# Nine transfers in place of one in a stream of weights, and four table rows on another queue

## The chip, the cores and the metric

The kernel runs on one core of a Trainium2 chip. The metric is the device time of one execution in microseconds (us); lower is better. Before the change the median of three runs is 419.34 us (419.34 to 419.83).

A core has five engines that the text speaks of by the names the profile gives them: PE (TensorE, matrix products), DVE (VectorE) and ACT (ScalarE) for elementwise work, POOL (GpSimd), and SP (SyncE), which here only issues transfers. Transfers between memory and the core's on-chip memory run on 16 DMA engines; an instruction on SP or POOL issues one, and it is then moved while the issuing engine goes on.

## The reference, cut to what matters

Linear attention with an elu feature map, followed by a spectral mixing layer: a real Fourier transform over the sequence, a complex 512 by 512 product for each of the 64 lowest modes, the inverse transform, and a channel product.

```python
def _attn_ref(q, k, v):                     # q, k, v: (8, 8, 576, 64) float32
    phi = lambda x: np.where(x > 0, x, np.exp(x) - 1.0) + 1.0
    q_p, k_p = phi(q), phi(k)
    kv = np.einsum('bhsd,bhse->bhde', k_p, v)
    z = np.sum(k_p, axis=2)
    num = np.einsum('bhsd,bhde->bhse', q_p, kv)
    den = np.einsum('bhsd,bhd->bhs', q_p, z)[..., None] + 1e-06
    return num / den

def _moe_ref(x, w_r, w_i, w_ch):            # x: (8, 576, 512); w_r, w_i: (64, 512, 512)
    X = np.fft.rfft(x, axis=1)
    Xr, Xi = np.real(X[:, :64]), np.imag(X[:, :64])
    Yr = np.einsum('bmd,mde->bme', Xr, w_r) - np.einsum('bmd,mde->bme', Xi, w_i)
    Yi = np.einsum('bmd,mde->bme', Xr, w_i) + np.einsum('bmd,mde->bme', Xi, w_r)
    Y = np.zeros_like(X); Y[:, :64] = Yr + 1j * Yi
    u = x + np.fft.irfft(Y, n=576, axis=1)
    return u + np.maximum(u @ w_ch, 0.0)
```

The weights `w_r` and `w_i` are 134 MB in float32, by far the largest input. They are read once and turned into bfloat16 on the way.

## The kernel before, in words

**Stages.** The first stage (about 0 to 113 us) does the attention of the eight batches and the forward transform. For each batch `load` (L169) brings q, k and v, `exps` and `features` build the feature maps, `turn_q` transposes q, `sum_kv` sums the products of k and v, `form_x` divides, `transform` multiplies by the forward table `fwd_sb`, and `place_x` puts the spectra where the mode products need them. The second stage (about 113 to 389 us) goes over the 64 modes in 32 pairs: `mode_pair(p)` (L528) multiplies the spectra by the weights of modes 2p and 2p + 1, 16 matmuls on one tile `P` (L498), and copies, picks and stores the result on chip. Between the pairs PE does slices of other work (`work_slot`): the attention rows again in float32, the inverse transform of the early modes, the channel product, and filler matmuls (`keep_warm`, L485). The last stage (to 418 us) adds the late modes and stores the output.

**The weights' transfers.** `w_load(p, half, ...)` (L104) issues one transfer on POOL: the real weights of a pair (half 0) or the imaginary ones (half 1). The tile has 128 rows; one half takes every other row, so a transfer is 64 rows of 16 x 512 elements, 16 KB each as bfloat16. A pair is multiplied when both its halves have landed. Five pairs (two in `wpool`, three in `wpre`) are loaded during the first stage, by `w_next` among the batches' loads. Later pairs go through `wpool` with two buffers: `w_get(p)` (L474) issues both halves of pair p once the products of pair p - 2, which had the buffer, are done. The last pair is loaded in pieces (`w_load_last`, L114).

**Queues and order.** Nearly all issues are in a hand-written order (`pin`), which holds for each engine. POOL issues k and v of batch 0, then q, k and v of batch 1, then makes the identity and the turning matrices (L311), then issues q of batch 2 and so on. SP issues q of batch 0 in two transfers (L177), then the forward table (L179): only 81 of its rows are stored, and `fold_table` (L324) makes the others on PE from these by symmetry, at 11.95 us and after, between `turn_q(0)` and `sum_kv(0)`. The stores of the last stage are SP's too.

**Completion counters.** Each transfer counts up a counter (a semaphore) when it has landed. The program as built gives POOL's transfers eight such counters in turn.

Of the kernel before, what the change touches and what calls it, by code (L numbers as in the profile page):

```python
# [33 lines left out]
def kernel(  # L34
# [10 lines left out]
    nc = tc.nc  # L45
# [6 lines left out]
    NJJ = 4  # L52
    NDW = 4 * NDC
# [12 lines left out]
    FROWS = S // 4 - 63  # L66
    fwd_dr = nc.inline_tensor(np.ascontiguousarray(fwd_np[:FROWS, :4]), name="dft_fwd")
# [6 lines left out]
    fwd_sb = const.tile([128, 5, 2 * NM], F16, name="fwd_sb")  # L74
# [23 lines left out]
    pin = tc.keep_in_program_order  # L98
# [2 lines left out]

    LAST = NM // 2 - 1

    def w_load(p: int, half: int, pool, tag: str, bufs: int):  # L104
        if half == 0:
            w_in[p] = pool.tile([128, NDW, D], BF16, tag=tag, bufs=bufs, name=f"w{p}")
        two = (moe_w_r, moe_w_i)[half][2 * p : 2 * p + 2]
        pin(
            nc.gpsimd.dma_start(  # L109
                out=w_in[p][half::2], in_=two.rearrange("g (r dc) e -> (g r) dc e", dc=NDW)  # L110
            )
        )

    def w_load_last(pool, tag: str, bufs: int):  # L114
        w_in[LAST] = pool.tile([128, NDW, D], BF16, tag=tag, bufs=bufs, name=f"w{LAST}")
# [23 lines left out]
    def w_next():  # L139
        p, half = pending.pop(0)  # L140
        pool, tag, bufs = (wpool, "w", W_KEEP) if p < n_keep else (wpre, "wp", W_PRE)
        w_load(p, half, pool, tag, bufs)
# [26 lines left out]
    def load(b):  # L169
        for nm, src in (("q", q), ("k", k), ("v", v)):  # L170
            rows_in = src[b].rearrange("h s d -> (h s) d").rearrange(
                "(hp r j) d -> r hp (j d)", r=128, j=2 * NJ
            )
            if (nm, b) == ("q", 0):
                for c in range(2):
                    t = sA.tile([128, 2, NJ * Dh], F32, tag="x16", bufs=2, name=f"q32_{c}")
                    pin(nc.sync.dma_start(out=t, in_=rows_in[:, :, c * NJ * Dh : (c + 1) * NJ * Dh]))  # L177
                    raw[nm, b, c] = t
                pin(nc.sync.dma_start(out=fwd_sb[0:FROWS, 0:NJJ, :], in_=fwd_dr.ap()))  # L179
                continue  # L180
            t = sA.tile([128, 2, 2 * NJ * Dh], F16, tag=f"{nm}16", bufs=2, name=f"{nm}16_{b}")
            pin(nc.gpsimd.dma_start(out=t, in_=rows_in))
            raw[nm, b] = t

    def heads(nm, b, c):
        if (nm, b) == ("q", 0):
            return raw[nm, b, c].rearrange("p o (j d) -> p o j d", d=Dh)
        return raw[nm, b].rearrange("p o (c j d) -> p c o j d", c=2, d=Dh)[:, c]
# [219 lines left out]
    def transform(b, dc):  # L408
# [17 lines left out]
        if dc == NDC - 1:  # L426
# [3 lines left out]
            pin(nc.scalar.mul(out=xv[:, :, 0, :], in_=xf[:, :, 1, :], mul=-SPEC))  # L430

    load(0)
    load(1)
    ones_where(id16, -1, 1, 0)
    make_turns()
# [4 lines left out]
    for b in range(B):  # L440
        if b + 2 < B:
            load(b + 2)
            if b % 2 == 1:
                w_next()
        turn_q(b, 0)
        turn_q(b, 1)
        if b == 0:
            fold_table()
        sum_kv(b)
        if b + 1 < B:  # L450
            for _ in features(b + 1):
                pass
        if b + 2 < B:
            exps(b + 2)
        for jj in range(NJJ + 1):
            form_x(b, jj)
            if b == 0 and jj == 0:
                make_place()
            if b > 1 and jj == 1:
                place_x(b - 2)  # L460
            if b > 0 and jj in (2, 3):
                transform(b - 1, jj - 2)
        if b > 0:
            transform(b - 1, 2)
            transform(b - 1, 3)
# [8 lines left out]
    def w_get(p: int):  # L474
        if p not in w_in and p == LAST:
            w_load_last(wpool, "w", W_KEEP)
        elif p not in w_in:
            for half in range(2):
                w_load(p, half, wpool, "w", W_KEEP)
        return w_in[p]  # L480
# [189 lines left out]
    def x_of(t: int):  # L670
        if t < B * NJJ:
            return x_main[t // NJJ][:, t % NJJ, :]
        i = t - B * NJJ
        return x_tail[i // 2][:, i % 2, :]
# [458 lines left out]
    def sums_of(n: int, tiles_of):  # L1133
        channels(n, tiles_of)
        add_inverse(n, 1, tiles_of)
        for i in tiles_of:
# [6 lines left out]
            out=x_of(0), in0=accs[0][:, 0], scalar=0.0, in1=x_of(0), op0=ALU.max, op1=ALU.add  # L1143
# [51 lines left out]
```

## Time and profile before

| what | us |
| --- | --- |
| median of three runs | 419.34 (419.34 to 419.83) |
| the profiled execution, whole | 419.94 |
| its span, first to last instruction | 418.2 |
| busy: PE / DVE / ACT / POOL | 295.0 / 240.2 / 153.2 / 61.3 |
| issue to landing, `w` from `in_moe_w_r_dram`, median | 12.5 |
| issue to landing, `w` from `in_moe_w_i_dram`, median | 16.8 |

The page that follows in parts comes from one profiled execution. Its third part lists the DMA queues: q0 holds what POOL issues, q1 what SP issues, q8 and q14 the fetches of instructions. Its fourth part is the chain of work that ended last, followed back from the end. A line of the fifth part reads: source line, engine, operation, tile written and tiles read, shape and count, then busy time and the mean of one in ns, then the idle time of that engine just before these instructions and what ended most of it. A line of the timeline reads: start, duration, engine, source line, operation, tiles, count, and in brackets the idle time before it and what ended it.

### The profile page before, as it was taken

What the parts mean: (1) busy time and instruction counts of PE and PEld (TensorE: products, weight loads), DVE (VectorE), ACT (ScalarE), POOL (GpSimd) and SP (SyncE); (2) the same over time, 40 slices, a digit from 0 to 9 for tenths busy, and PEclk for the clock granted to TensorE, in tenths of its full rate; (3) what the DMA queues carried; (4) which work ended last, traced back from release to release, by engine and by line L of the source; (5) the groups of instructions that cost most, each with busy time, mean ns of one, the idle gap of its engine ahead of it and who ended that gap; (6) DMA issues with size and microseconds to landing.
All of it is one profiled execution on the core that took longest, in us unless ns stands there. A gap on an engine that the chain in (4) does not pass through costs nothing.

```text
span 418.2 us, 6982 instructions
## 1 busy us (share of the span) xinstructions
PE 295.0 (71%) x2890; PEld 158.9 (38%) x2890; DVE 240.2 (57%) x533; ACT 153.2 (37%) x226; POOL 61.3 (15%) x110
## 2 busy tenths in 40 slices
PE   0279999999674455444435676978796967998992
PEld 0167777777411222212122232333342422453431
DVE  4779879995437474455536453564454534522794
ACT  4667767954200001000000233334352522331682
POOL 6222222300020111111111111111111111130200
PEclk9999999989755655556665589999897988899997
DMA  8999999999999999999999999999999999998698
GB/s 216 212 212 214 211 219 205 222 215 220 212 215 218 213 221 212 216 217 216 218 216 215 219 212 216 218 215 217 216 215 218 215 215 219 215 210 172 210 401 344
DMA packets 16564, 92.86 MB, mean 222 GB/s; under 512 B 2069, under 2 KB 2790, under 8 KB 12374
## 3 DMA queue, kind: packets, MB, share of 16 engines
q0 software_dynamic: 12656, 81.53, 93.8%
q1 hardware_dynamic: 3878, 10.90, 6.9%
q8 instruction: 22, 0.36, 0.3%
q14 instruction: 8, 0.07, 0.0%
HBM read 163.66 MB, written 9.44 MB: 414 GB/s over the span
## 4 chain that ended last, share of the span: by engine, by line
DMA 55%; PE 25%; DVE 10%; ACT 3%; issue 3%; POOL 3%; ACTq 0%; POOLq 0%
DMA w<-in_moe_w_i_dram 52%; PE P L498 5%; PE kvp L258 5%; DVE x_main L965 4%; DMA k<-in_k_dram 3%; DVE x L294 3%; PE xf L417 2%; PE qTp L238 2%; PE xp L385 2%; POOL w L109 2%; PE num L156 1%; PE zl L485 1%; PE z L858 1%; ACT qT L245 1%; PE xf L422 1%
## 5 line engine op out<-in xcount | busy, mean ns | idle before, releaser
L498 PE MATMUL P<-w,xz 128*32 128x512 bf16 x496 | 49.2, 537 | 71.7 <-DMA w<-in_moe_w_i_dram 69.4
L109 POOL DMA_DIRECT2D w<-in_moe_w_r_dram x31 | 17.2, 553 | 247.9 <-PE P L498 246.2
L515 ACT CAST ys<-P 128x512 f16<-128x512 f32 x15 | 8.8, 586 | 118.1 <-PE P L498 112.3
L498 PEld LDWEIGHTS <-xz 128*32 128x32 bf16 x496 | 12.9, 117 | 93.8 <-DMA w<-in_moe_w_i_dram 77.3
L513 DVE CAST ys<-P 128x512 f16<-128x512 f32 x17 | 11.8, 692 | 58.0 <-PE P L498 58.0
L838 PE MATMUL eps<-wch,xTw 128*128 128x512 f16 x144 | 42.0, 420 | 0.0
L819 DVE TENSOR_TENSOR x_main<-ya,x_main 128x512 f32<-128x512 f32 x32 | 22.0, 689 | 20.5 <-PE ya L815 20.3
L821 ACT CAST x16w<-x_main 128x512 f16<-128x512 f32 x32 | 19.8, 618 | 37.1 <-DVE x_main L819 35.4
L258 PE MATMUL kvp<-vpad,ke 32*128 32x130 f16 x576 | 24.0, 265 | 8.5 <-ACT qT L245 8.5
L846 ACT CAST E<-eps 128x512 f16<-128x512 f32 (+1 forms) x40 | 21.2, 540 | 22.4 <-PE eps L838 22.4
L769 PE MATMUL nw<-kv_diag,qT 128*128 128x130 f16 (+1 forms) x160 | 24.6, 297 | 6.4 <-DVE x_tail L782 3.2
L258 PEld LDWEIGHTS <-ke 32*128 32x128 f16 x576 | 22.2, 117 | 10.0 <-issue 9.6
L508 DVE COPY xz<-xt_c 64x256 bf16<-64x256 bf16 x62 | 22.9, 369 | 2.2 <-PE P L498 1.4
L294 DVE TENSOR_TENSOR x<-num,rd 128x512 f16<-128x512 f32 x32 | 22.1, 691 | 1.1
L238 PE MATMUL qTp<-id,qe 128*128 128x128 f16 x144 | 15.2, 289 | 10.1 <-DVE qe L222 9.6
L769 PEld LDWEIGHTS <-qT 128*128 128x128 f16 (+1 forms) x160 | 14.5, 134 | 19.9 <-issue 11.4
L156 PE MATMUL num<-kv_sb,qT 64*128 64x65 f16 (+1 forms) x320 | 16.3, 219 | 5.7 <-DVE x L294 3.3
L245 ACT COPY qT<-qTp 128x1152 f16<-128x1152 f16 x16 | 19.6, 1293 | 2.0 <-PE qTp L238 1.5
L782 DVE TENSOR_TENSOR x_main<-nw,rd 128x256 f32<-128x256 f32 x32 | 11.2, 415 | 15.8 <-PE nw L769 15.8
L830 DVE COPY xTw<-xTp 128x512 f16<-128x512 f16 x36 | 15.0, 416 | 6.8 <-PE xTp L828 6.8
L838 PEld LDWEIGHTS <-xTw 128*128 128x128 f16 x144 | 13.7, 107 | 11.8 <-issue 4.7
L204 ACT ACTIVATE ke<-k 128x2304 f16<-128x2304 f16 x8 | 16.9, 2112 | 2.6 <-DMA k<-in_k_dram 2.6
(153 smaller groups left out, 525.2 us busy)
## 6 DMA issues: line engine op xcount, KB each, us to landing
w<-in_moe_w_r_dram POOLq DMA_DIRECT2D x31, 1024.0 KB, 12.5
w<-in_moe_w_i_dram POOLq DMA_DIRECT2D x31, 1024.0 KB, 16.8
out_dram<-x_main SPq DMA_DIRECT2D x14, 512.0 KB, 3.5
k<-in_k_dram POOLq DMA_DIRECT2D x8, 576.0 KB, 12.0
v<-in_v_dram POOLq DMA_DIRECT2D x8, 576.0 KB, 12.4
q<-in_q_dram POOLq DMA_DIRECT2D x7, 576.0 KB, 11.7
q<-in_q_dram SPq DMA_DIRECT2D x2, 576.0 KB, 4.4
w<-in_moe_w_r_dram POOLq DMA_DIRECT2D x2, 512.0 KB, 11.5
```

The costliest lines, as they stand in the source:

```text
L109: nc.gpsimd.dma_start(out=w_in[p][half::2], in_=two.rearrange("g (r dc) e -> (g r) dc e", dc=NDW))
L156: mm = nc.tensor.matmul(num[hpo][orow, c0 : c0 + 65], qT[rows, hpp, h2, cols], kv_sb[rows, hpp, h2, :])
L238: nc.tensor.transpose(qT_ps[:, j], phi["q", b][:, c, j].rearrange("p o d -> p (o d)"), id16,)
L245: nc.scalar.copy(out=qT[:, :, c * NJ : (c + 1) * NJ], in_=qT_ps.rearrange("p j x -> p x j"))
L258: nc.tensor.matmul(kv_ps[:, h2, 0:130], phi["k", b][r0 : r0 + 32, j // NJ, j % NJ].rearrange("p o d -> p (o d)"), vp[r0 : r0 + 32, :, j, 0 ...
L294: nc.vector.tensor_tensor(out=dst.rearrange("p (o c d) -> p o c d", o=2, c=4), in0=nv[:, :, :, 0:64], in1=rden.unsqueeze(3).broadcast_to([ ...
L498: nc.tensor.matmul(P[c : c + n, :], x, w[:, dc, :], start=(dc < NDC), stop=(dc >= n_dc - NDC), tile_position=(0, c), skip_group_check=True,)
L508: pin(nc.vector.tensor_copy(out=xz[p % 2][HALVES[h], :, h, :], in_=src))
L769: nc.tensor.matmul(num[c][orow, h2 * 130 : h2 * 130 + 130], qT[:, c, h2, rows_of(jj, BASE[b % 2])], kv_diag[:, b, c, h2].rearrange("p o n ...
L819: pin(nc.vector.tensor_tensor(out=x, in0=acc, in1=x, op=ALU.add))
L838: nc.tensor.matmul(e_ps, xT[:, c, :], wch16[:, c, :], start=(c == 0), stop=(c == NDC - 1))
L846: pin(nc.scalar.copy(out=dst, in_=e_ps[:, cols]))
```

## The change

Two edits. In the first, `W_SHARES` names one half of one pair, the imaginary weights of pair 24, and `w_load` issues it as nine transfers: one of 48 rows and eight of 2 rows. All other halves stay one transfer of 64 rows. In the second, SP's transfer of the forward table carries 77 rows in place of 81, and the other four are issued by POOL, right behind v of batch 0.

```diff
+    W_SHARES = {(24, 1): (48,) + (2,) * 8}
+
     def w_load(p: int, half: int, pool, tag: str, bufs: int):
         if half == 0:
             w_in[p] = pool.tile([128, NDW, D], BF16, tag=tag, bufs=bufs, name=f"w{p}")
         two = (moe_w_r, moe_w_i)[half][2 * p : 2 * p + 2]
-        pin(
-            nc.gpsimd.dma_start(
-                out=w_in[p][half::2], in_=two.rearrange("g (r dc) e -> (g r) dc e", dc=NDW)
-            )
-        )
+        rows_in, r0 = two.rearrange("g (r dc) e -> (g r) dc e", dc=NDW), 0
+        for n in W_SHARES.get((p, half), (64,)):
+            pin(nc.gpsimd.dma_start(out=w_in[p][half::2][r0 : r0 + n], in_=rows_in[r0 : r0 + n]))
+            r0 += n
...
-                pin(nc.sync.dma_start(out=fwd_sb[0:FROWS, 0:NJJ, :], in_=fwd_dr.ap()))
+                pin(nc.sync.dma_start(out=fwd_sb[0 : FROWS - 4, 0:NJJ, :], in_=fwd_dr.ap()[0 : FROWS - 4]))
                 continue
             t = sA.tile([128, 2, 2 * NJ * Dh], F16, tag=f"{nm}16", bufs=2, name=f"{nm}16_{b}")
             pin(nc.gpsimd.dma_start(out=t, in_=rows_in))
             raw[nm, b] = t
+            if (nm, b) == ("v", 0):
+                r = slice(FROWS - 4, FROWS)
+                pin(nc.gpsimd.dma_start(out=fwd_sb[r, 0:NJJ, :], in_=fwd_dr.ap()[r]))
```

## The prediction

> **What bounds the kernel now.** I read the page first, for the engine that never rests and the chain that ends last.
>
> ```profile
> span 418.2 us, 6982 instructions
> ...
> DMA  8999999999999999999999999999999999998698
> ...
> q0 software_dynamic: 12656, 81.53, 93.8%
> q1 hardware_dynamic: 3878, 10.90, 6.9%
> q8 instruction: 22, 0.36, 0.3%
> ...
> DMA 55%; PE 25%; DVE 10%; ACT 3%; issue 3%; POOL 3%; ACTq 0%; POOLq 0%
> ...
> L498 PE MATMUL P<-w,xz 128*32 128x512 bf16 x496 | 49.2, 537 | 71.7 <-DMA w<-in_moe_w_i_dram 69.4
> L109 POOL DMA_DIRECT2D w<-in_moe_w_r_dram x31 | 17.2, 553 | 247.9 <-PE P L498 246.2
> ```
>
> The DMA row stands at 9 from the second slice to the 36th, and 55% of the chain is transfers: from 117 to 389 us the kernel is one stream of weights on GpSimd's queue, and TensorE waits for it (69.4 of L498's 71.7 us of idle time). Whatever delays this stream delays the end; the 28 us behind it are a fixed tail. Next the timeline of TensorE and GpSimd around pair 24, whose second half is cut up:
>
> ```profile
> 299.28 1.05 PE L498 MATMUL P<-w,xz 128*32 128x512 bf16 x16 [2.47 <-DMA w<-in_moe_w_i_dram]
> ...
> 300.65 0.54 POOL L109 DMA_DIRECT2D w<-in_moe_w_r_dram  x1 [8.57 <-PE P L498]
> 301.19 0.55 POOL L109 DMA_DIRECT2D w<-in_moe_w_i_dram  x1
> ...
> 309.10 1.05 PE L498 MATMUL P<-w,xz 128*32 128x512 bf16 x16 [1.02 <-DMA w<-in_moe_w_i_dram]
> ...
> 310.46 0.54 POOL L109 DMA_DIRECT2D w<-in_moe_w_r_dram  x1 [8.73 <-PE P L498]
> ...
> 318.78 1.90 PE L498 MATMUL P<-w,xz 128*32 128x512 bf16 x16 [3.34 <-DMA w<-in_moe_w_i_dram]
> ```
>
> Pair 22 is multiplied at 299.28, its buffer is free at 300.65, and pair 24 is issued there. Pair 23 lands at 309.10 and pair 25 is issued at 310.46, while pair 24 is still moving until 318.78: the queue holds about 8 us of work whenever an issue comes, so it never empties. That reserve is what the change can spend.
>
> The trace's DMA records (one per packet) add two things. A row of a half is one packet of 16 KB and 1.227 us, four rows per engine, and successive halves complete 4.85 us apart. And the 16 engines are not level: the completion marks of one transfer lie 0.7 us apart at the start, 3.28 us at pair 24, 3.65 us at the last pairs. The 22 instruction fetches of q8 (16 KB, 0.89 to 0.98 us each) each go through one engine and, as I read it, leave it behind. A landing is that of the slowest engine.
>
> Last, how GpSimd's transfers wait for each other. In the program as built they take eight completion counters in turn, and a transfer waits until the former user of its counter, eight transfers earlier, has landed, unless something before it proves that. The trace has this wait:
>
> ```profile
> 74.70 0.58 POOL L109 DMA_DIRECT2D w<-in_moe_w_r_dram  x1
> 76.52 0.74 POOL L109 DMA_DIRECT2D w<-in_moe_w_i_dram  x1 [1.25 <-DMA q<-in_q_dram]
> 78.93 0.54 POOL L109 DMA_DIRECT2D w<-in_moe_w_r_dram  x1 [1.67 <-DMA k<-in_k_dram]
> 81.70 0.54 POOL L109 DMA_DIRECT2D w<-in_moe_w_i_dram  x1 [2.23 <-DMA v<-in_v_dram]
> ```
>
> The buffers of these weights are free; what ends each wait is a q, k or v load issued eight transfers before. It costs nothing there, because the queue is full.
>
> **The table's four rows.** SP's third transfer shrinks from 81 to 77 rows; GpSimd gets a transfer more, between v of batch 0 and q of batch 1. Nearest rows for its issue: 0.60 us (the four-row L1118, 1.20 for two) and 0.73 us (the q, k, v loads). So q, k and v of the next batch, two `affine_select`s' worth of work (L311) and q of batch 2 are issued up to 0.7 us later. These loads sit behind a queue that lands one load per 2.79 us from 9.4 us on (k of batch 1 is issued at 3.60 and lands at 17.72), so nothing is late. The rows themselves land behind v of batch 0, at about 12.3 us, where the first table matmul (L330) ran at 11.95: TensorE starts it 0.3 us later, covered because VectorE takes the result only at 14.45, behind v's copy (L228), and TensorE's next work is at 21.07. The packets cost the stream 0.05 us. From both sides: -0.1 to +0.7 if that cover failed. I take 0.
>
> **The cut half.** Removed: one issue of 0.55 us and 64 rows. Added: nine issues, the same 64 rows. Bytes are equal, and I take the 16 pieces' rows as evenly spread, so each engine still has 3 + 1 rows. Issues: the four-piece row of L121 has 2.21 us for four, so 0.55 each; GpSimd idles 8.7 us here. What is new are the waits. As built, pieces 1 to 4 wait for nothing, piece 5 for pair 23's first half (304.2), piece 6 for its second (309.1), piece 7 for pair 24's first half (318.78 - 4.85 = 313.93), and piece 8 for the 48-row transfer itself. Behind piece 8 on GpSimd stands pair 25, which was issued at 310.46 before. So:
>
> 1. The 48 rows land one row before the old landing: 318.78 - 1.23 = 317.55.
> 2. GpSimd wakes 0.25 us after TensorE for the same landing (rows below: 377.82 and 378.07): piece 8 is issued at 317.80.
> 3. Pair 25's first half follows one issue later, at 318.35, instead of 310.46.
> 4. From the start of an issue to its first packet on an empty queue: 1.56 us (L1067) and 1.66 (L1118), issue rows below against the DMA records. I take 1.6: 319.95.
> 5. Piece 8's own row: 317.80 + 1.6 + 1.23 = 320.63, so pair 24 lands there, 1.85 late, and two engines start pair 25 at 320.63.
>
> ```profile
> 377.82 1.05 PE L498 MATMUL P<-w,xz 128*32 128x512 bf16 x16 [0.60 <-DMA w<-in_moe_w_i_dram]
> 378.07 0.55 POOL L121 DMA_DIRECT2D w<-in_moe_w_i_dram  x1 [4.04 <-DMA w<-in_moe_w_i_dram]
> ...
> 387.49 0.64 POOL L1067 DMA_DIRECT2D YZ_all<-rows_ahead  x1 [8.88 <-DMA w<-in_moe_w_i_dram]
> ...
> 389.89 1.20 POOL L1118 DMA_DIRECT2D YZ_all<-last_z  x2 [1.76 <-ACT last_z L1113]
> ```
>
> The slowest engine had begun pair 25 at 318.78; the most advanced one at 318.78 - 3.28 = 315.50. All now begin at 319.95: 1.17 late for the slowest, 4.45 for the most advanced. The engines are level again, which takes away the lag of the past, and the lag to come starts from zero: fetches at 329.9, 352.0 and 376.1 us put 0.9 to 0.95 on one engine each, where before they raised the spread only from 3.28 to 3.65. End of the stream: 4.45 + 0.95 - 3.65 = +1.75 us; with a fetch on one of piece 8's engines +2.4. What follows is late by the same: pair 26 waits for pair 24's products, issued 2 us later, with pair 25 moving until 329.7, so no second gap. TensorE's surplus waits for nine counters are some 0.04 us each (the POOLq semaphore instructions) and long satisfied. I take **+1.8 us**.
>
> Step 4 is the least known. Nearest rows on both sides: 1.43 us (SP's first issue at 0.81, first packet at 2.24) and 4.5 us (GpSimd's first load, issued 1.33, first packet 5.86, at start-up). I take the two of the tail, whose queue was warm and empty. That gives +1.6 to +4.7. The Trainium skill, "DMA: Bandwidth & Descriptors", section "Latency and other measured facts", puts the first byte from GpSimd at about 1 us; by that figure the sum would be +1.2. This trace says 1.6.
>
> On the profiled execution, 418.2 us of span and 419.94 in all (1.7 around it), that is 421.7; it lies 0.6 over the median of 419.34, on which I put the forecast: 419.34 + 1.8 = **421.1 us**.
>
> **Rivals.**
> - *The gap is hidden*: same. If waking, two issues and the first packet together take under 2 us instead of 2.4, and later fetches strike engines that are not last, the sum is at most +0.8: 419.3 to 420.1. For it: the slowest engine has only 1.17 us of gap. Against it: the same steps measured in the tail.
> - *Two engines take all pieces.* If each two-row transfer goes to the same two engines, these have 3 + 8 rows. A most advanced engine ends them at 314.30 + 8 x 1.23 = 324.1 (piece 8 arrives at 319.4, in time): +5.4, less 0.4 of lag, 424.3; the slowest one: +8.6, 427.9. The records show four-row transfers starting on four engines (the tail's L1118), but not whether the next one takes other engines. The Trainium skill, same page, "Why a DMA increments its semaphore by 16 and not by 1", describes both: engines in turn from a cursor, and an exception with a fixed ceil(rows/16) per engine; the second would give this rival, and no row here decides.
> - *The cut spares the slowest engine*: faster. If the pieces miss the engine that is 3.28 us behind, it has three rows instead of four, and pair 24 could land at 317.55. It decides only if pair 25's first packet is there 1.23 us after the 48 rows, that is if piece 8 doesn't wait for them; then the stream gains 1.2: 418.1. Against it: the wait is in the program as built, and eight times two rows are just 16 engines.
> - *Every piece pays its own start.* If the eight pieces went one behind the other at 0.25 + 0.55 + 1.6 + 1.23 = 3.6 us, the last seven would cost 25 us: 444. Against it: halves complete 4.85 us apart, with no start between them, and six pieces are queued early.
>
> **How the numbers follow.** Forecast 0.74, hidden 0.10, two engines 0.09, faster 0.05, every piece 0.02. The forecast's own range is 420.4 to 422.4; the 8-in-10 range takes in half of the hidden case, the long first packet and the cheaper end of the two engines: 419.9 to 424.4. A change of 0.2% (0.84 us) is about what can be told from none: faster 0.05, same 0.11, slower 0.84.
>
> **What would show it.** In the changed trace: GpSimd's eighth piece and pair 25 issued near 318 us with a wait for the imaginary weights, instead of 310.5; a dip in the DMA row at 318 to 320; pair 24's products at about 320.6 and pair 25's near 330 instead of 328.5; the spread of completion marks under 1 us behind pair 24; the tail equally long. I am wrong if pair 25 is issued at 310.5, if the DMA row has no dip, if marks of two engines come some 5 us behind the rest, or if the first table matmul's delay reaches VectorE.

## The result, and the profile after

The changed kernel takes 426.17 us (median of 4 runs, 425.81 to 426.6) against 419.36 before (4 runs, 419.34 to 419.83): a ratio of 1.016, 95% interval 1.0143 to 1.0178. That is 6.8 us slower, where 1.8 was forecast, and it lies outside the forecast range (419.9 to 424.4).

The page of the changed kernel, the lines that answer to those of before:

```profile
span 423.8 us, 6998 instructions
...
DMA  8999999999999999999999999999978999998598
...
q0 software_dynamic: 12928, 81.54, 92.7%
...
DMA 59%; PE 19%; DVE 10%; issue 4%; ACT 3%; POOL 3%; ACTq 0%; POOLq 0%
...
L502 PE MATMUL P<-w,xz 128*32 128x512 bf16 x496 | 49.5, 540 | 78.7 <-DMA w<-in_moe_w_i_dram 76.5
...
L112 POOL DMA_DIRECT2D w<-in_moe_w_r_dram x31 | 17.1, 553 | 236.5 <-PE P L502 233.7
```

The span grew by 5.6 us. TensorE's idle time before the products (L502, formerly L498) grew by 7.0, all of it waiting for imaginary weights, and the DMA row, level before, has a dip (7, 8) in slices 30 and 31, that is from 307 to 328 us. The timeline there, the products of pairs 22 to 25 and GpSimd's issues; TensorE's other work between them is left out:

```profile
299.79 1.05 PE L502 MATMUL P<-w,xz 128*32 128x512 bf16 x16
301.15 0.54 POOL L112 DMA_DIRECT2D w<-in_moe_w_r_dram  x1 [7.80 <-PE P L502]
301.69 2.53 POOL L112 DMA_DIRECT2D w<-in_moe_w_i_dram  x5
304.84 0.51 POOL L112 DMA_DIRECT2D w<-in_moe_w_i_dram  x1 [0.62 <-DMA w<-in_moe_w_r_dram]
309.47 1.90 PE L502 MATMUL P<-w,xz 128*32 128x512 bf16 x16 [2.00 <-DMA w<-in_moe_w_i_dram]
309.71 0.50 POOL L112 DMA_DIRECT2D w<-in_moe_w_i_dram  x1 [4.36 <-DMA w<-in_moe_w_i_dram]
314.60 0.50 POOL L112 DMA_DIRECT2D w<-in_moe_w_i_dram  x1 [4.39 <-DMA w<-in_moe_w_r_dram]
318.24 0.64 POOL L112 DMA_DIRECT2D w<-in_moe_w_i_dram  x1 [3.14 <-DMA w<-in_moe_w_i_dram]
318.87 0.56 POOL L112 DMA_DIRECT2D w<-in_moe_w_r_dram  x1
319.42 0.55 POOL L112 DMA_DIRECT2D w<-in_moe_w_i_dram  x1
325.18 1.90 PE L502 MATMUL P<-w,xz 128*32 128x512 bf16 x16 [7.90 <-DMA w<-in_moe_w_i_dram]
...
334.62 1.05 PE L502 MATMUL P<-w,xz 128*32 128x512 bf16 x16 [1.02 <-DMA w<-in_moe_w_i_dram]
```

The waits are those that were forecast: the last pieces are issued one by one, each behind a landing, and pair 25 at 318.87 in place of 310.46. But pair 24 is multiplied only at 325.18, 6.9 us after the issue of its last piece began. The windows of the same execution show what moves meanwhile (columns: stretch, length, busy time and count of PE, weight load, DVE, ACT and POOL, clock, DMA share, GB/s):

```profile
314.00:316.00 2.00, 2.00 (x18) 1.32 (x16) 1.74 (x6) 1.10 (x2) 0.50 (x1) 1.00 0.49 99
316.00:318.00 2.00, 1.28 (x7) 0.33 (x4) 2.00 (x5) 0.74 (x2) 0.00 (x0) 1.00 0.22 41
318.00:320.00 2.00, 0.00 (x0) 0.00 (x0) 0.77 (x3) 0.88 (x2) 1.74 (x3) 0.86 0.16 33
320.00:322.00 2.00, 0.00 (x0) 0.00 (x0) 0.00 (x0) 0.00 (x0) 0.00 (x0) 0.50 1.04 156
322.00:324.00 2.00, 0.00 (x0) 0.00 (x0) 0.00 (x0) 0.00 (x0) 0.00 (x0) 0.50 1.04 221
```

From 318 to 320 us a share of 0.16 is two or three engines of 16. From 320 to 324 the DMA engines are all busy again (1.04) while no engine computes: that is pair 25 on most engines, and it doesn't help, because pair 24 isn't complete. The DMA records carry no engine numbers, but a packet that starts where another ends can be followed as one engine's, and two such chains are late. Starts of their 16 KB packets from the first piece on, in us on the records' clock (about 10.15 ahead of the timeline, as the marks compare with the counters), each preceded by the 4-byte completion mark of the transfer before:

```
one engine    324.337 325.565 326.793 328.021 329.250 330.478 331.706 332.934
another       325.216 326.444 327.672 328.900 330.129 331.357 332.585 333.813
```

Eight pieces, eight rows on each of two engines, 1.228 us apart. Every two-row transfer went to the same two engines. They hold 3 + 8 rows, the other fourteen 3. The second one's last mark is at 335.02, 324.9 on the timeline: pair 24's landing. The eighth piece's counter says the same: it takes one mark from each of the 16 engines, fourteen of them at 319.77 to 319.95 and the last two at 324.14 and 325.09.

### The profile page after: what moved, and what is told of

It reads as the page before. It is cut to its first block, busy times and chain, and to the rows that moved or that the text cites. A ratio compares the mean times of both kernels' runs of the same rounds, so it can differ in the third digit from the quotient of the medians.

```text
span 423.8 us, 6998 instructions
## 1 busy us (share of the span) xinstructions
PE 291.9 (69%) x2890; PEld 157.3 (37%) x2890; DVE 240.1 (57%) x533; ACT 153.1 (36%) x226; POOL 66.1 (16%) x119
## 4 chain that ended last, share of the span: by engine, by line
DMA 59%; PE 19%; DVE 10%; issue 4%; ACT 3%; POOL 3%; ACTq 0%; POOLq 0%
DMA w<-in_moe_w_i_dram 49%; DMA k<-in_k_dram 6%; PE P L502 6%; DVE x_main L969 4%; DMA w<-in_moe_w_r_dram 3%; PE kvp L262 3%; DVE x L298 3%; PE eps L842 2%; POOL w L112 1%; PE qTp L242 1%; PE xf L421 1%; PE xp L389 1%; ACT ke L208 1%; PE acc L896 1%; ACT qT L249 1%
## 5 line engine op out<-in xcount | busy, mean ns | idle before, releaser
L502 PE MATMUL P<-w,xz 128*32 128x512 bf16 x496 | 49.5, 540 | 78.7 <-DMA w<-in_moe_w_i_dram 76.5
L502 PEld LDWEIGHTS <-xz 128*32 128x32 bf16 x496 | 13.6, 117 | 100.2 <-DMA w<-in_moe_w_i_dram 62.8
L842 PE MATMUL eps<-wch,xTw 128*128 128x512 f16 x144 | 43.6, 433 | 0.0
L262 PE MATMUL kvp<-vpad,ke 32*128 32x130 f16 x576 | 22.7, 255 | 8.1 <-ACT qT L249 8.1
L262 PEld LDWEIGHTS <-ke 32*128 32x128 f16 x576 | 20.9, 112 | 9.6 <-issue 9.2
L112 POOL DMA_DIRECT2D w<-in_moe_w_i_dram x39 | 21.2, 544 | 16.9 <-DMA w<-in_moe_w_i_dram 7.5
```

The lines of the kernel that those rows point to most:

```text
L112: pin(nc.gpsimd.dma_start(out=w_in[p][half::2][r0 : r0 + n], in_=rows_in[r0 : r0 + n]))
L262: nc.tensor.matmul(kv_ps[:, h2, 0:130], phi["k", b][r0 : r0 + 32, j // NJ, j % NJ].rearrange("p o d -> p (o d)"), vp[r0 : r0 + 32, :, j, 0 ...
L502: nc.tensor.matmul(P[c : c + n, :], x, w[:, dc, :], start=(dc < NDC), stop=(dc >= n_dc - NDC), tile_position=(0, c), skip_group_check=True,)
L842: nc.tensor.matmul(e_ps, xT[:, c, :], wch16[:, c, :], start=(c == 0), stop=(c == NDC - 1))
```

## The experiments

Two theories were set against each other. Theory 1: always the same two engines take the two-row pieces, and their extra rows are the loss. Theory 2: the waits for landings, with a slow start of every small transfer behind them, are the loss, wherever the rows go.

**Each edit alone.** First the table rows without the cut:

```diff
-    W_SHARES = {(24, 1): (48,) + (2,) * 8}
+    W_SHARES = {}
```

> Only the four table rows go through GpSimd's queue; no half is cut. Both theories put the whole loss on the cut half, so both expect no change: 419.4 us within 0.8, ratio 0.998 to 1.002. If the table rows had a share in it, some of the 6.8 us would appear here.

Measured: 419.74 us against 419.57, ratio 1.0009 (1.0 to 1.0019). Then the cut without the table rows:

```diff
-                pin(nc.sync.dma_start(out=fwd_sb[0 : FROWS - 4, 0:NJJ, :], in_=fwd_dr.ap()[0 : FROWS - 4]))
+                pin(nc.sync.dma_start(out=fwd_sb[0:FROWS, 0:NJJ, :], in_=fwd_dr.ap()))
...
-            if (nm, b) == ("v", 0):
-                r = slice(FROWS - 4, FROWS)
-                pin(nc.gpsimd.dma_start(out=fwd_sb[r, 0:NJJ, :], in_=fwd_dr.ap()[r]))
```

> The cut half alone, the table as before. Both theories expect the whole loss: 425.5 to 427 us, ratio 1.015 to 1.018, pair 24 multiplied near 325 us and the 14 other engines idle before it.

Measured: 426.03 us, ratio 1.0154 (1.0139 to 1.017). The whole loss is the cut's. The following kernels all have the table as before.

**The waits without the crowding.** The same nine transfers in the same order, but each piece is 16 rows by two of the 16 column blocks:

```diff
+        if (p, half) == (24, 1):
+            pin(nc.gpsimd.dma_start(out=w_in[p][half::2][0:48], in_=rows_in[0:48]))
+            for i in range(8):
+                c = slice(2 * i, 2 * i + 2)
+                pin(nc.gpsimd.dma_start(out=w_in[p][half::2][48:64, c], in_=rows_in[48:64, c]))
+            return
```

> Nine transfers, the same order, the same bytes and the same chain of counter waits, but each of the eight pieces is 16 rows of two columns' worth (2 KB packets), so that it has rows for all 16 engines. Theory 1 (two engines take all two-row pieces; the waits alone cost a gap of 1.2 us for the slowest engine): 420.5 to 421.7 us, piece 8 and pair 25 issued near 318 us as in the changed kernel, pair 24 multiplied near 320.5. Theory 2 (the waits and a slow start of each small transfer make the loss, wherever the rows go): 425 to 427 us, pair 24 again near 325.

Measured: 423.12 us, ratio 1.0088 (1.0071 to 1.0105): +3.5 us, between the two expectations. Its timeline:

```profile
317.74 0.48 POOL L114 DMA_DIRECT2D w<-in_moe_w_i_dram  x1 [3.11 <-DMA w<-in_moe_w_i_dram]
317.82 1.64 PE L502 MATMUL P<-w,xz 128*32 128x512 bf16 x14 [2.45 <-DMA w<-in_moe_w_i_dram]
318.25 0.56 POOL L116 DMA_DIRECT2D w<-in_moe_w_r_dram  x1
...
319.94 0.61 PE L502 MATMUL P<-w,xz 128*32 128x512 bf16 x2 [0.48 <-DMA w<-in_moe_w_i_dram]
...
332.04 1.90 PE L502 MATMUL P<-w,xz 128*32 128x512 bf16 x16 [5.63 <-DMA w<-in_moe_w_i_dram]
```

The eighth piece and pair 25 are issued as in the changed kernel, and pair 24 is done at 320.5 (14 of its matmuls need only the other columns and run earlier). So a small transfer isn't slow by itself, and theory 2 falls as the account of pair 24's delay. But pair 25 is multiplied at 332.04, 3.5 us later than before (328.52), and the records say from what. Its first packets start at 319.85, 1.07 after the moment at which the slowest engine began them before (318.78), as computed. These 16 packets then take 1.7 to 2.3 us, median 2.17, where nearly every later one takes 1.23: 0.9 more, which no step of the prediction had. And one engine falls 1.2 behind the rest before the pair is in, where a fetch of instructions stands in the records; with all engines level there is no slack for it. The three make 3.2 of the 3.5 (an estimate from one execution).

**The crowding without the waits.** Four-row pieces, five transfers, none behind a landing:

```diff
-    W_SHARES = {(24, 1): (48,) + (2,) * 8}
+    W_SHARES = {(24, 1): (48,) + (4,) * 4}
```

> The half as 48 rows and four times 4 rows: five transfers, none of which waits for another transfer's landing, so pair 25 is issued near 310.5 us and no engine goes empty. Theory 1 with always the same four engines: these have 3 + 4 rows, three more than an even share (3.7 us); taken from engines that were up to 3.3 us ahead, the loss is 0.5 to 3.7 us: 419.9 to 423.1. Theory 2, or a distribution that goes round the engines: 419.0 to 419.8, no change.

Measured: 423.17 us, ratio 1.0085 (1.007 to 1.01): +3.6, 0.07 above the upper end of theory 1's span.

```profile
309.07 1.05 PE L499 MATMUL P<-w,xz 128*32 128x512 bf16 x16 [2.14 <-DMA w<-in_moe_w_i_dram]
310.43 0.56 POOL L112 DMA_DIRECT2D w<-in_moe_w_r_dram  x1 [6.75 <-PE P L499]
...
321.79 1.90 PE L499 MATMUL P<-w,xz 128*32 128x512 bf16 x16 [4.81 <-DMA w<-in_moe_w_i_dram]
```

Pair 25 is issued on time (310.43), the queue never runs dry, and pair 24 is still 3.0 us late. In the records four engines carry one row of each of the four pieces, at 1.228 us. One of the four was 2.2 us behind the most advanced engine; its three extra rows (3.7) end 2.8 after the slowest engine of the stream, which stood at 3.1.

**How the two combine.** In the changed kernel the waits empty fourteen engines, but the crowded two never pause. Then the waits should add nothing there, and each piece less should save exactly one row:

```diff
-    W_SHARES = {(24, 1): (48,) + (2,) * 8}
+    W_SHARES = {(24, 1): (48,) + (2,) * 5 + (6,)}
```

> 48 rows, five times 2 and once 6: seven transfers, and pair 25's first half no longer waits behind the landing of the 48 rows (only for pair 24's first half, near 314 us), so the queue never runs dry. Theory 1 says the two engines hold 3 + 6 rows in place of 3 + 8, and that the waits add nothing in the changed kernel because these two engines never idle: 426.1 - 2 x 1.23 = 423.7 us (423.2 to 424.2). If the waits have a share of their own in the 6.7 us (alone they cost 3.5), it is lower: 420.5 to 422.5.

Measured: 423.71 us, ratio 1.0098 (1.0084 to 1.0112), 2.46 us under the changed kernel (2.65 when each is taken against the runs of before beside it); two rows are 2.46. Its windows, stretches as above:

```profile
314.00:316.00 2.00, 1.57 (x10) 0.62 (x9) 2.00 (x6) 0.44 (x1) 0.55 (x1) 1.00 0.72 148
316.00:318.00 2.00, 0.00 (x0) 0.00 (x0) 1.06 (x3) 1.18 (x3) 0.00 (x0) 0.98 1.05 172
318.00:320.00 2.00, 0.00 (x0) 0.00 (x0) 0.00 (x0) 0.00 (x0) 0.55 (x1) 0.50 1.08 229
320.00:322.00 2.00, 0.00 (x0) 0.00 (x0) 0.00 (x0) 0.00 (x0) 0.00 (x0) 0.50 0.97 205
```

The dip is all but gone: 0.72 from 314 to 316, where 0.49 stood, then 1.05 and 1.08, where 0.22 and 0.16 stood. That the queue never runs dry was expected and isn't quite so, but the time follows the rows alone. The gap of some 2.5 to 6.4 us on fourteen engines of the changed kernel, from their last row of the 48 to their first packet of pair 25, was worth nothing there, because it lay beside the two that were late.

**Where the lead went.** Seven extra rows are 8.6 us, but the loss is 6.5 to 6.8. If the rest is the lead of the two engines over the slowest one, it can be spent once only:

```diff
-    W_SHARES = {(24, 1): (48,) + (2,) * 8}
+    W_SHARES = {(24, 1): (48,) + (2,) * 8, (27, 1): (48,) + (2,) * 8}
```

> The same cut in pair 24 and again in pair 27. Theory 1: the first cut used up the lead of the two engines (8.6 us of extra rows less some 2.6 of lead); at pair 27 these two are the slowest themselves, so the second cut costs its full seven rows, 8.6 us: 434.0 to 435.5 us. If each cut simply cost the same: 432.3 to 433.3.

Measured: 435.65 us, ratio 1.0381 (1.0365 to 1.0396). The second cut costs 9.6 us against 6.5 for the first alone. It is dearer, as theory 1 says, and the time lies 0.15 us above the upper end of what was expected. In the records the later of the two engines is the last of the 16 to finish pair 27's first half, so there is no lead left. Pair 27's products start 15.6 us later than before, where pair 26's were 6.4 later: 9.2 at the cut itself. Another 1.4 comes at pair 28 (17.0 later), whose products wait for no weights: TensorE is busy up to them without a break from 372.04, at a granted clock of 0.50 to 0.56 since pair 27's products. At the last pairs 16.3 is left.

**A control, and an attempt to gain.** If n rows always go to the same n engines, then a cut can also take load off the others. First 48 and 16 rows, both even:

```diff
-    W_SHARES = {(24, 1): (48,) + (2,) * 8}
+    W_SHARES = {(24, 1): (48, 16)}
```

> Control: the half as 48 and 16 rows, both spread over all 16 engines, no wait for a landing. Cutting by itself costs one issue under the cover of the queue: 419.0 to 420.0 us, no change.

Measured: 419.71 us against 419.55, ratio 1.0002 (0.9993 to 1.0011). Cutting alone is free. Then 48, 8 and 8:

```diff
-    W_SHARES = {(24, 1): (48,) + (2,) * 8}
+    W_SHARES = {(24, 1): (48, 8, 8)}
```

> The half as 48, 8 and 8 rows: three transfers, no wait for a landing. If a transfer of n rows always goes to the same first n engines (theory 1), eight engines get five rows and eight get three. That is 1.23 us more for the first eight and 1.23 less for the others: the end of the stream moves by -1.2 us if all the engines that lag (by 2.0 to 3.8 us) are among the last eight, by +1.2 if the slowest is among the first eight, and by something between if the first eight lag by 2.2 at most: 418.2 to 420.8. If the second eight rows went to the other eight engines: no change, 419.2 to 419.8.

Measured: 420.98 us, ratio 1.0029 (1.002 to 1.0038): +1.4, a little over the dearest case, one more row on the slowest engine. It isn't the "no change" that the second eight rows on the other eight engines would give, and the gain isn't there. But the trace doesn't bear out that the slowest engine is among the eight that get more. Pair 24's products start 10.13 us after pair 23's (309.52 and 319.65), where it was 9.68: 0.45 more, not a row of 1.23. In the records the engine that finishes pair 24's first half last has three rows behind it and then begins pair 25, so in this execution it got less. The rest of the loss appears only at pair 26 (1.4 later than before, pair 25 was 0.4 later), in whose first half one mark comes 1.1 behind the other fifteen, with a fetch of instructions in the records shortly before. An engine close behind the slowest that gets more rows, and then a fetch, would do that; it isn't shown. In none of these runs did a transfer of fewer than 16 rows load the other eight and spare these eight, and no version faster than before came of it.

## Why the prediction was wrong

- *What bounds the kernel*: right. The weights' stream sets the end; what delayed pair 24 by 6.4 us (318.78 to 325.18) is still 5.6 at the end of the span.
- *The table's four rows*: right. The first table matmul waits 0.33 us for them and starts at 12.34 instead of 11.95 (0.3 later was forecast), and the edit alone costs nothing that can be measured.
- *The waits (steps 1 to 4)*: right in kind and close in time. Pieces 5 to 8 and pair 25 stand close to where they were put, piece 8 at 318.24 against 317.80, pair 25 at 318.87 against 318.35; 0.5 of that was there at pair 22. From pair 25's issue to its first packet it is 1.61 us against 1.6.
- *"I take the 16 pieces' rows as evenly spread, so each engine still has 3 + 1 rows"*: this step failed, and it is the cause of the miss. In step 5 it made piece 8's row the only one behind its issue (320.63). In truth each of the two engines had eight rows in line, without a pause, up to 324.9. The prediction's own sign of being wrong, marks of two engines some 5 us behind the rest, is there: 4.2 and 5.1.
- *The rival "two engines take all pieces"* named the mechanism at a chance of 0.09, with 424.3 us if the two are the most advanced engines and 427.9 if they include the slowest. They were in between: the records put the later of the two 0.93 us behind the most advanced engine, where the slowest one of that execution stood at 3.84, so 8.6 - 2.9 = 5.7 us at pair 24's landing. The records of before had shown four-row transfers on four engines; that the next ones might take the same four was left open, and the even case was chosen without a row for it. It is there that the sum and the range should have gone by the dearer bound. The Trainium skill, "DMA: Bandwidth & Descriptors", "Why a DMA increments its semaphore by 16 and not by 1", has both a cursor and fixed shares. The runs here agree with the fixed shares: eight two-row transfers stood in line on two engines, not on sixteen.
- *The size of the gap*: for the waits alone 1.8 us was worked out, 3.5 is measured. Missing were the slow first packets of 16 engines that start together (0.9), and a fetch put as 0.95 that left its engine 1.2 behind. In the changed kernel neither counted.

## What to carry to other kernels

When a stream of transfers is the bound, count rows per DMA engine, not bytes: the landing is that of the engine with the most, and the price of a cut is its extra rows less the lead that this engine happens to have, which can be spent once. On a queue like this one, cut a transfer only into pieces whose row count is a multiple of the number of engines (16 here); 48 + 16 was free, 48 + 8 x 2 cost 6.8 us with the same bytes. And count how many transfers are in flight between an issue and the reuse of its counter: here the ninth waited for a landing, which emptied the queue even where the rows were even (+3.5 us).

## What the runs showed of the hardware that was not expected

- Transfers of 2 rows went to the same two engines eight times running (one row per engine and transfer, 1.228 us apart), and transfers of 4 rows to the same four, four times running.
- After the queue had run dry, the first 16 KB packet of each engine took 1.7 to 2.3 us (median 2.17) with pieces spread evenly, and 1.6 to 2.5 in the changed kernel, against 1.227 in the stream.
- The 16 engines drift apart by 3 to 4 us over the stream (3.84 at pair 24 of the changed kernel), and a lead hides extra rows: there 2.9 of 8.6 us, on the later of the two crowded engines.
